# Short first and last token blocks, half a batch of attention ahead of the feed-forward on VectorE, and an in-place maximum in PSUM

## The chip, the cores and the metric

The kernel runs on one core of one Trainium2 chip. The core has TensorE (PE in the profile, with its weight loads shown apart as PEld), VectorE (DVE), ScalarE (ACT), GpSimd (POOL) and SyncE (SP). Each takes its instructions in the order in which they were issued and waits on semaphores. The metric is the device time of one launch in microseconds (us).

## The reference

The inputs are q, k and v, each of 8 batches, 8 heads, 576 positions and 64 features in float32, and two matrices, `w_in` (512 x 2048) and `w_out` (2048 x 512). What is computed, cut to what matters:

```
mask   = abs(pos_q - pos_k) <= 32
scores = where(mask, q @ k.T / sqrt(64), -1e9)
attn   = softmax(scores) @ v                      # per batch and head
x      = attn, heads side by side                 # 4608 tokens x 512
h      = x @ w_in                                 # 4608 x 2048
g      = h if h >= 1, 0 if h <= -1, else (h+1)**2 / 4
out    = g @ w_out                                # 4608 x 512, float32
```

Both kernels use g = min(r, 1) * max(h, r) with r = relu((h+1)/2).

## The kernel before

**Attention.** Two heads make a pair `i` (32 pairs, 4 to a batch); two pairs make a group of four heads, `m` (16 groups, 2 to a batch). `load_qk(m)` fetches q and k of a group on POOL's DMA queue, which also converts float32 to bf16. A partition of `qn` holds nine successive positions of a head, so one row in DRAM is 2304 bytes; `kn` is fetched 64 features at a time, rows of 256 bytes, and so is v (`load_v(i)`, into `vz`, whose other half stays zero). `relay(m)` on POOL reorders `qn` into `qj`. `tpose(m, t)` turns five or four 128 x 128 pieces of `qj` (t = 0, 1) or of `kn` (t = 2, 3) on PE; ACT copies q to `qT`, and DVE copies k into the block-diagonal tile `kz`. `scores(i, g)` multiplies three blocks of 64 keys by the up to 128 queries that can see them, takes exp on ACT and multiplies by the band mask `maskp` on POOL, giving `pt`. `pv(i, hf)` computes for one half (288 positions) the sums of the weights, `dn`, and the weighted v, `nm`, on PE; ACT makes 1/dn with Ln and Exp (`lr`, `rc`), and DVE multiplies (`mul`) into `xT`, the transposed x of all tokens.

**Feed-forward.** Nine blocks of 512 tokens, 16 steps each. In step f PE makes `hp`, 128 of the 2048 features for the block's tokens (four matmuls of 512 columns); ACT makes `rr` = r; DVE writes the maximum of `hp` and `rr` to `yy` in SBUF (L248) and then min(rr, 1) * `yy` to `gT` (L249). In the same step PE does four of the 64 matmuls by `w_out` of the block before (`op`); every fourth step ACT copies a finished `op` to `osb`, and SP's queue stores it.

**Order.** All engines run in program order, written out in one loop over steps `a`. `att_s`, `att_x` and `att_r` say at which step a score group, a transpose, a `pv` or a relay is done; `loads` does so for later loads. The feed-forward begins at step OFF = 29, so 29 steps of attention alone come before it. `hp` and the tiles shared by `tp` and `sc` have two PSUM buffers each, `nm` and `dn` one. PE's order within a step is hp, scores, op, transpose, pv.

Of the kernel before, what the change touches and what calls it, by code (L numbers as in the profile page):

```python
# [15 lines left out]
def kernel(  # L16
# [14 lines left out]

    nc = tc.nc
# [5 lines left out]
    TB = 512  # L38
    NBLK = NT // TB

# [4 lines left out]
    def pcol(c, qq):  # L45
        return qq if c % 2 == 0 else S + qq - 32

    PW = 2 * S - 64
    GROUPS = [(0, 2, 4), (6, 8, 1), (3, 5, 7)]
# [5 lines left out]
    ptp = ctx.enter_context(tc.tile_pool(name="ptp", bufs=3))  # L55
# [18 lines left out]
    vz = [const.tile([128, NC, 128], BF, name=f"vz{i}") for i in range(8)]  # L74
# [5 lines left out]

    def load_qk(m):
        b, qd = divmod(m, 2)
        qn[m] = qkn.tile([128, 2, S], BF, name="qn")
        kn[m] = qkn.tile([128, NC, 2, D], BF, name="kn")
        for g in range(2):
            h0 = 4 * qd + 2 * g
            nc.gpsimd.dma_start(out=qn[m][64 * g:64 * g + 64],
                                in_=q[b, h0:h0 + 2].rearrange("h (p j) d -> p h (j d)", j=NC))
        for g in range(2):
            for h in range(2):  # L90
                nc.gpsimd.dma_start(out=kn[m][64 * g:64 * g + 64, :, h],  # L91
                                    in_=k[b, 4 * qd + 2 * g + h].rearrange("(c p) d -> p c d", p=64))

    def load_v(i):
        b, hp = divmod(i, H // 2)
        for h in range(2):
            nc.gpsimd.dma_start(  # L97
                out=vz[i % 8][64 * h:64 * h + 64, :, 64 * h:64 * h + 64],
                in_=v[b, 2 * hp + h].rearrange("(c p) d -> p c d", p=64))

    nc.scalar.preload_act_table_set("natural_log_exp_and_others")
    load_qk(0)
    for t in kz:
        nc.vector.memset(t.rearrange("p c h r -> p (c h r)").bitcast(FP), 0.0)
    for i in range(8):
        nc.vector.memset(vz[i].rearrange("p c d -> p (c d)").bitcast(FP), 0.0)  # L106
    make_identity(nc, ident)
    for i in range(4):
        load_v(i)
    load_qk(1)  # L110
# [3 lines left out]
    for h in range(2):  # L114
        r = slice(64 * h, 64 * h + 64)
        nc.gpsimd.memset(ones2[r, r], 1.0)
        nc.gpsimd.affine_select(out=mask1[r], in_=mask1[r], compare_op=ALU.is_ge, fill=0.0, base=0,
                                channel_multiplier=-1, pattern=[[1, 128]])
        nc.gpsimd.affine_select(out=mask1[r], in_=mask1[r], compare_op=ALU.is_ge, fill=0.0, base=64,
                                channel_multiplier=1, pattern=[[-1, 128]])  # L120
    for c in range(NC):
        q0, q1 = qrange(c)
        j0 = q0 - (64 * c - 32)
        nc.vector.tensor_copy(maskp[:, pcol(c, q0):pcol(c, q0) + q1 - q0], mask1[:, j0:j0 + q1 - q0])
    nc.gpsimd.dma_start(out=w_in, in_=moe_w_in.rearrange("(ko ki) f -> ki ko f", ki=128))
    load_qk(2)
    for i in range(4, 8):
        load_v(i)
    nc.gpsimd.dma_start(out=w_out, in_=moe_w_out.rearrange("(ko ki) f -> ki ko f", ki=128))


    qj, qT = {}, {}

    def relay(m):

        qj[m] = qjp.tile([128, NC, 2, D], BF, name="qj")
        nc.gpsimd.tensor_copy(qj[m].rearrange("p j h d -> p h j d"),  # L137
                              qn[m].rearrange("p h (j d) -> p h j d", d=D))
# [3 lines left out]
    def tpose(m, t):  # L142

        src, (j0, j1) = (qj if t < 2 else kn)[m], TJ[t % 2]
        ps = ps_s.tile([128, 5, 128], BF, name="tp", tag="sc")
        if t == 0:
            qT[m] = qtp.tile([128, 2, S], BF, name="qT")
        for j in range(j0, j1):
            nc.tensor.transpose(ps[:, j - j0], src[:, j].rearrange("p h d -> p (h d)"), ident)  # L149
        n = j1 - j0  # L150
        if t < 2:
            for g in range(2):
                nc.scalar.copy(  # L153
                    qT[m][:, g].rearrange("d (p j) -> d p j", j=NC)[:, :, j0:j1],
                    ps[:, :n].rearrange("d j (g p) -> d g p j", g=2)[:, g])
        else:
            for h in range(2):
                for g in range(2):
                    r = slice(64 * h, 64 * h + 64)
                    nc.vector.tensor_copy(kz[2 * (m % 2) + g][r, j0:j1, h],  # L160
                                          ps[r, :n].rearrange("d c (g p) -> d g c p", g=2)[:, g])
# [3 lines left out]
    def scores(i, g):  # L165
# [5 lines left out]
        first = None  # L171
        for c in GROUPS[g]:
            q0, q1 = qrange(c)
            nc.tensor.matmul(ps[:, off:off + q1 - q0], kz[2 * (m % 2) + gg][:, c].rearrange("d h r -> d (h r)"),  # L174
                             qT[m][:, gg, q0:q1], start=True, stop=True)
            if first is None:
                first = pcol(c, q0)
            off += q1 - q0
        seg = slice(first, first + off)

        nc.scalar.activation(pt[i][:, seg], ps[:, :off], AF.Exp, scale=D ** -0.5)  # L181
        nc.gpsimd.tensor_mul(pt[i][:, seg], pt[i][:, seg], maskp[:, seg])  # L182

    def pv(i, hf):
# [3 lines left out]
        o0, o1 = max(lo, 32), min(hi, S - 32)  # L188
        nc.tensor.matmul(dn, ones2, pt[i][:, lo:hi], start=True, stop=False)  # L189
        nc.tensor.matmul(dn[:, o0 - lo:o1 - lo], ones2, pt[i][:, pcol(1, o0):pcol(1, o1)], start=False, stop=True)  # L190
# [6 lines left out]
        for n, (c, q0, q1) in enumerate(parts):  # L197
            nc.tensor.matmul(nm[:, q0 - lo:q1 - lo], vz[i % 8][:, c], pt[i][:, pcol(c, q0):pcol(c, q1)],  # L198
                             start=n == 0, stop=n == len(parts) - 1, skip_group_check=True)

# [8 lines left out]
        return mul  # L209


    A0 = 9
    att_s, att_x, att_r = {}, {}, {}
    for m in range(NP // 2):
        for t in range(4):
            att_x[8 * m + 2 * t] = ("t", m, t)
        att_r[8 * m - 1] = m
    for i in range(NP):
        for g in range(3):
            att_s[A0 + 4 * i + g] = (i, g)  # L220
        for hf in range(2):
            att_x[A0 + 4 * i + 4 + 2 * hf] = ("v", i, hf)
    OFF = A0 + 4 * 3 + 6 + 2
    loads = {}
    for m in range(3, NP // 2):
        loads.setdefault(8 * m - 16, []).append((load_qk, m))
    for i in range(8, NP):
        loads.setdefault(4 * i - 14, []).append((load_v, i))

    gT = {}  # L230
    mul = None
    for a in range(-1, OFF + 16 * (NBLK + 1)):
        mm = a - OFF
        blk, f = divmod(mm, 16)
        for fn, arg in loads.get(a, []):
            fn(arg)
        if 0 <= mm and blk < NBLK:
            if f == 0:
                gT[blk] = gtp.tile([128, 16, TB], BF, name="gT")
            hp = ps_h.tile([128, TB], FP, name="hp")  # L240
            for kk in range(4):
                nc.tensor.matmul(hp, w_in[:, kk, 128 * f:128 * f + 128], xT[:, kk, TB * blk:TB * blk + TB],  # L242
                                 start=kk == 0, stop=kk == 3)

            rr = ewp.tile([128, TB], FP, name="rr")
            yy = ewp.tile([128, TB], FP, name="yy")
            nc.scalar.activation(rr, hp, AF.Relu, scale=0.5, bias=0.5)  # L247
            nc.vector.tensor_max(yy, hp, rr)  # L248
            nc.vector.scalar_tensor_tensor(gT[blk][:, f], rr, 1.0, yy, op0=ALU.min, op1=ALU.mult)  # L249
        if mul:  # L250
            mul()
            mul = None
        if a in att_s:
            scores(*att_s[a])
        if 1 <= blk <= NBLK and mm >= 0:
            tt, f0 = divmod(f, 4)
            if f0 == 0:
                op = ps_o.tile([128, DM], FP, name="op")
            for ff in range(4 * f0, 4 * f0 + 4):
                nc.tensor.matmul(op, gT[blk - 1][:, ff, 128 * tt:128 * tt + 128], w_out[:, ff],  # L260
                                 start=ff == 0, stop=ff == 15)
            if f0 == 3:
                osb = osp.tile([128, DM], FP, name="osb")
                nc.scalar.copy(osb, op)  # L264
                t0 = TB * (blk - 1) + 128 * tt
                nc.sync.dma_start(out=out[t0:t0 + 128, :], in_=osb)
        if a in att_r:
            relay(att_r[a])
        if a in att_x:
            kind, i, t = att_x[a]  # L270
            if kind == "t":
                tpose(i, t)
            else:
                mul = pv(i, t)
# [30 lines left out]
```

## Time and profile before

| | |
|---|---|
| median of 3 runs | 393.26 us (392.73 to 393.27) |
| the profiled execution | 393.38 us, of which its span is 391.7 us |
| granted TensorE clock, mean | 0.987 |
| busy: PE, DVE, ACT, POOL | 82%, 74%, 56%, 56% of the span |

The span is the time from the first to the last recorded event; 1.68 us of the profiled execution lie around it. [...] In rows of the profile `out<-in` names tiles, `x` is a count, and what stands in square brackets is the engine's idle time ahead of the instruction and what ended it.

### The profile page before, as it was taken

What the parts mean: (1) busy time and instruction counts of PE and PEld (TensorE: products, weight loads), DVE (VectorE), ACT (ScalarE), POOL (GpSimd) and SP (SyncE); (2) the same over time, 40 slices, a digit from 0 to 9 for tenths busy, and PEclk for the clock granted to TensorE, in tenths of its full rate; (3) what the DMA queues carried; (4) which work ended last, traced back from release to release, by engine and by line L of the source; (5) the groups of instructions that cost most, each with busy time, mean ns of one, the idle gap of its engine ahead of it and who ended that gap; (6) DMA issues with size and microseconds to landing.
All of it is one profiled execution on the core that took longest, in us unless ns stands there. A gap on an engine that the chain in (4) does not pass through costs nothing.

```text
span 391.7 us, 6070 instructions
## 1 busy us (share of the span) xinstructions
PE 322.4 (82%) x2136; PEld 177.9 (45%) x2176; DVE 289.0 (74%) x501; ACT 219.8 (56%) x469; POOL 219.9 (56%) x288
## 2 busy tenths in 40 slices
PE   0000765677699999999999999999999999999995
PEld 0000554444355555555555555555555544444442
DVE  6100332699899999999999999999998877787720
ACT  1000564666677767675867777776766644434421
POOL 8947889996776858694958768642422200000000
PEclk9999995899999999999999999999999999999999
DMA  9999996992939678794939395830000100101012
GB/s 81 99 195 141 172 163 47 73 78 18 77 26 120 77 71 93 67 96 51 104 42 104 45 128 65 83 43 27 28 28 28 54 28 27 54 28 52 29 55 80
DMA packets 88190, 28.18 MB, mean 72 GB/s; under 512 B 76896, under 2 KB 83040, under 8 KB 88160
## 3 DMA queue, kind: packets, MB, share of 16 engines
q0 software_dynamic: 82976, 18.36, 53.2%
q1 hardware_dynamic: 5184, 9.44, 6.4%
q8 instruction: 17, 0.28, 0.3%
q14 instruction: 13, 0.11, 0.1%
HBM read 36.70 MB, written 9.44 MB: 118 GB/s over the span
## 4 chain that ended last, share of the span: by engine, by line
PE 71%; POOL 11%; DVE 9%; DMA 3%; issue 2%; ACT 2%; another core or an unknown queue 1%; ACTq 0%; POOLq 0%
PE op L260 30%; PE hp L242 28%; DMA w_in<-in_moe_w_in_dram 3%; POOL vz L97 3%; PE nm L198 3%; DVE gT L249 3%; PE tp L149 3%; POOL pt L182 3%; PE sc L174 3%; DVE yy L248 3%; POOL kn L91 3%; PE dn L189 2%; PE dn L190 2%; DVE vz L106 1%; DVE xT L208 1%
## 5 line engine op out<-in xcount | busy, mean ns | idle before, releaser
L242 PE MATMUL hp<-xT,w_in 128*128 128x512 bf16 x555 | 146.0, 379 | 4.2 <-DVE xT L208 3.0
L260 PE MATMUL op<-w_out,gT 128*128 128x512 bf16 x557 | 142.3, 379 | 0.7
L249 DVE SCALAR_TENSOR_TENSOR gT<-rr,yy 128x512 bf16<-128x512 f32 x144 | 130.3, 905 | 5.1
L182 POOL TENSOR_TENSOR pt<-pt,maskp 128x352 bf16<-128x352 bf16 (+1 forms) x96 | 85.6, 907 | 79.2 <-ACT pt L181 78.8
L247 ACT ACTIVATE rr<-hp 128x512 f32<-128x512 f32 x144 | 86.1, 598 | 76.7 <-PE hp L242 71.6
L248 DVE TENSOR_TENSOR yy<-hp,rr 128x512 f32<-128x512 f32 x144 | 99.2, 689 | 26.7 <-ACT rr L247 24.4
L260 PEld LDWEIGHTS <-gT 128*128 128x128 bf16 x576 | 53.5, 98 | 51.7
L242 PEld LDWEIGHTS <-w_in 128*128 128x128 bf16 x576 | 51.9, 98 | 43.2 <-issue 0.2
L97 POOL DMA_DIRECT2D vz<-in_v_dram x64 | 48.7, 773 | 8.2 <-DMA w_in<-in_moe_w_in_dram 7.4
L160 DVE COPY kz<-tp 64x320 bf16<-64x320 bf16 (+1 forms) x128 | 33.2, 298 | 25.8 <-PE tp L149 25.3
L149 PE MATMUL tp<-ident,qj 128*128 128x128 bf16 x144 | 15.2, 242 | 44.6 <-POOL qj L137 43.8
L153 ACT COPY qT<-tp 128x320 bf16<-128x320 bf16 (+1 forms) x64 | 24.8, 454 | 47.9 <-PE tp L149 47.7
L91 POOL DMA_DIRECT2D kn<-in_k_dram x64 | 47.9, 791 | 0.9 <-PE tp L149 0.9
L181 ACT ACTIVATE pt<-sc 128x352 bf16<-128x352 f32 (+1 forms) x96 | 45.0, 468 | 2.0 <-PE sc L174 1.8
L208 DVE TENSOR_TENSOR xT<-nm,rc 128x288 bf16<-128x288 f32 x64 | 28.8, 449 | 16.8 <-ACT rc L204 16.8
L203 ACT ACTIVATE lr<-dn 128x288 f32<-128x288 f32 x64 | 26.5, 414 | 19.8 <-PE dn L190 19.8
L174 PEld LDWEIGHTS <-kz 128*128 128x128 bf16 x288 | 25.0, 104 | 25.6 <-issue 6.4
L149 PEld LDWEIGHTS <-qj 128*128 128x128 bf16 x144 | 10.6, 108 | 52.9 <-POOL qj L137 49.4
L174 PE MATMUL sc<-qT,kz 128*128 128x128 bf16 (+1 forms) x288 | 33.2, 228 | 1.6 <-ACT pt L181 1.2
L198 PE MATMUL nm<-pt,vz 128*128 128x128 bf16 (+2 forms) x320 | 27.7, 221 | 7.5 <-DVE xT L208 7.5
L264 ACT COPY osb<-op 128x512 f32<-128x512 f32 x36 | 21.1, 587 | 19.4 <-PE op L260 16.6
L198 PEld LDWEIGHTS <-vz 128*128 128x128 bf16 x320 | 22.2, 103 | 17.8 <-issue 12.5
(26 smaller groups left out, 158.8 us busy)
## 6 DMA issues: line engine op xcount, KB each, us to landing
out_dram<-osb SPq DMA_DIRECT2D x36, 256.0 KB, 2.0
qn<-in_q_dram POOLq DMA_DIRECT2D x32, 144.0 KB, 3.6
kn<-in_k_dram POOLq DMA_DIRECT2D x64, 72.0 KB, 4.4
vz<-in_v_dram POOLq DMA_DIRECT2D x64, 72.0 KB, 3.0
w_in<-in_moe_w_in_dram POOLq DMA_DIRECT2D x1, 2048.0 KB, 12.8
w_out<-in_moe_w_out_dram POOLq DMA_DIRECT2D x1, 2048.0 KB, 15.0
```

Source lines behind the costliest of these rows:

```text
L91: nc.gpsimd.dma_start(out=kn[m][64 * g:64 * g + 64, :, h], in_=k[b, 4 * qd + 2 * g + h].rearrange("(c p) d -> p c d", p=64))
L97: nc.gpsimd.dma_start(out=vz[i % 8][64 * h:64 * h + 64, :, 64 * h:64 * h + 64], in_=v[b, 2 * hp + h].rearrange("(c p) d -> p c d", p=64))
L149: nc.tensor.transpose(ps[:, j - j0], src[:, j].rearrange("p h d -> p (h d)"), ident)
L174: nc.tensor.matmul(ps[:, off:off + q1 - q0], kz[2 * (m % 2) + gg][:, c].rearrange("d h r -> d (h r)"), qT[m][:, gg, q0:q1], start=True, st ...
L181: nc.scalar.activation(pt[i][:, seg], ps[:, :off], AF.Exp, scale=D ** -0.5)
L182: nc.gpsimd.tensor_mul(pt[i][:, seg], pt[i][:, seg], maskp[:, seg])
L198: nc.tensor.matmul(nm[:, q0 - lo:q1 - lo], vz[i % 8][:, c], pt[i][:, pcol(c, q0):pcol(c, q1)], start=n == 0, stop=n == len(parts) - 1, ski ...
L242: nc.tensor.matmul(hp, w_in[:, kk, 128 * f:128 * f + 128], xT[:, kk, TB * blk:TB * blk + TB], start=kk == 0, stop=kk == 3)
L247: nc.scalar.activation(rr, hp, AF.Relu, scale=0.5, bias=0.5)
L248: nc.vector.tensor_max(yy, hp, rr)
L249: nc.vector.scalar_tensor_tensor(gT[blk][:, f], rr, 1.0, yy, op0=ALU.min, op1=ALU.mult)
L260: nc.tensor.matmul(op, gT[blk - 1][:, ff, 128 * tt:128 * tt + 128], w_out[:, ff], start=ff == 0, stop=ff == 15)
```

## The change

1. **Block sizes.** The nine blocks of 512 tokens become `sizes = [256] + [512] * 8 + [256]`.
2. **Attention ahead of the feed-forward.** Instead of 29 loop steps, a hand-written stretch does the first half (`hf = 0`) of the four pairs of batch 0. Relays, the copies into `kz` (`zfill`) and the mask multiplications run on DVE there, and during the first block (t = 0, steps 0 to 15) too; from block 1 on, relays and mask multiplications are on POOL again. Attention of batch 0's second half and of batch 1 is spread over block 0, batch b (2 to 7) over block b - 1.
3. **Score groups** become (0, 2, 4), (1, 3) and (6, 8, 5, 7), so that the first half needs only the first two.
4. **Loads.** For groups m = 0 to 3 k is fetched like q, in rows of 2304 bytes, relayed (`kj`), transposed to `kT` and copied to `kz`. A group's q (and k) is one DMA over 128 partitions instead of two of 64. v is fetched per group. `w_in` comes in two pieces (columns 0 to 511 early, the rest later, four DMAs each) and `w_out` in four. Later q and k loads are issued up to 38 steps ahead.
5. **Maximum in place.** DVE writes the maximum over `hp` in PSUM (L363); `yy` is gone, and L364 reads `hp`. The `hp` buffer comes free after L364 instead of after the maximum.
6. `zero` clears only the halves of `kz` and `vz` that no load fills, and clears `vz` later.

The core of the diff:

```
-    GROUPS = [(0, 2, 4), (6, 8, 1), (3, 5, 7)]
+    GROUPS = [(0, 2, 4), (1, 3), (6, 8, 5, 7)]
...
+    LONG = 4
     def load_qk(m):
...
+            if nm == "kn" and m >= LONG:
+                t = dst[m] = qkn.tile([128, NC, 2, D], BF, name="kn", tag="kn")
...
+            t = dst[m] = qkn.tile([128, 2, S], BF, name=nm, tag=nm)
+            rows = src[b, 4 * qd:4 * qd + 4].rearrange("(h g) s d -> h (g s) d", g=2)
+            nc.gpsimd.dma_start(out=t, in_=rows.rearrange("h (x j) d -> x h (j d)", j=NC))
...
+    load_v(0, 0, 5)
+    load_v(1, 0, 5)
+    load_w_in(0, 512)
     load_qk(2)
+    load_qk(3)
+    load_v(0, 5, NC)
+    load_v(1, 5, NC)
+    load_w_in(512, DFF)
+    load_v(2)
+    load_v(3)
+    for n in range(4):
+        load_w_out(n)
...
+    def zfill(m, g, eng):
+        for h in range(2):
+            r = slice(64 * h, 64 * h + 64)
+            eng.tensor_copy(kz[2 * (m % 2) + g][r, :, h], kT[m][r, g].rearrange("d (c r) -> d c r", r=64))
...
-        nc.gpsimd.tensor_mul(pt[i][:, seg], pt[i][:, seg], maskp[:, seg])
+        eng.tensor_mul(pt[i][:, seg], pt[i][:, seg], maskp[:, seg])
...
+    sizes = [256] + [512] * 8 + [256]
...
+        eng = V if t == 0 else P
...
-            nc.vector.tensor_max(yy, hp, rr)
-            nc.vector.scalar_tensor_tensor(gT[blk][:, f], rr, 1.0, yy, op0=ALU.min, op1=ALU.mult)
+            nc.vector.tensor_max(hp[:, :n], hp[:, :n], rr[:, :n])
+            nc.vector.scalar_tensor_tensor(gT[t][:, f, :n], rr[:, :n], 1.0, hp[:, :n], op0=ALU.min, op1=ALU.mult)
```

**Order on POOL's queue at the start.** Before, from the load of `w_in` on (`vz_112` to `vz_115` are the v tiles of batch 1, `qj` the relayed q):

```order
L125 DMA w_in<-in_moe_w_in_dram 128x4x2048
L87 DMA qn<-in_q_dram 64x2x576 x2
L91 DMA kn<-in_k_dram 64x9x64 x4
L97 DMA vz_112<-in_v_dram 64x9x64 x2
L97 DMA vz_113<-in_v_dram 64x9x64 x2
L97 DMA vz_114<-in_v_dram 64x9x64 x2
L97 DMA vz_115<-in_v_dram 64x9x64 x2
L129 DMA w_out<-in_moe_w_out_dram 128x16x512
L137 COPY qj<-qn 128x2x9x64 x2
```

In the changed kernel the same stretch, from the first piece of `w_in` on (`vz_108` and `vz_109` are v of batch 0, `vz_110` and `vz_111` of batch 1; the `qn` after `w_out` is that of group 4, the first of batch 2):

```order
L117 DMA w_in<-in_moe_w_in_dram 64x2x512 x4
L99 DMA qn<-in_q_dram 128x2x576
L99 DMA kn<-in_k_dram 128x2x576
L99 DMA qn<-in_q_dram 128x2x576
L99 DMA kn<-in_k_dram 128x2x576
L111 DMA vz_108<-in_v_dram 64x4x64 x4
L111 DMA vz_109<-in_v_dram 64x4x64 x4
L117 DMA w_in<-in_moe_w_in_dram 64x2x1536 x4
L108 DMA vz_110<-in_v_dram 64x18x64 x2
L108 DMA vz_111<-in_v_dram 64x18x64 x2
L121 DMA w_out<-in_moe_w_out_dram 128x4x512 x4
L99 DMA qn<-in_q_dram 128x2x576
```

The relay no longer stands behind `w_out` on POOL, and q of group 4 stands behind everything else.

**Order on DVE ahead of the feed-forward.** Before, after the memsets (`mask_99` is the band of one block, `tp` the transposed k):

```order
L124 COPY maskp<-mask_99 128x96
L124 COPY maskp<-mask_99 128x128 x7
L124 COPY maskp<-mask_99 128x96
L160 COPY kz_104<-tp 64x5x64
L160 COPY kz_105<-tp 64x5x64
```

In the changed kernel, after the memsets of `kz`:

```order
L169 COPY qj<-qn 128x2x9x64
L169 COPY kj<-kn 128x2x9x64
L198 COPY kT<-tp 128x128x5
L198 COPY kT<-tp 128x128x4
L203 COPY kz_104<-kT 64x9x64 x2
L267 COPY maskp<-mask_99 128x96
L267 COPY maskp<-mask_99 128x128 x7
L267 COPY maskp<-mask_99 128x96
L220 TENSOR_TENSOR pt<-pt,maskp 128x352
L220 TENSOR_TENSOR pt<-pt,maskp 128x256
L169 COPY qj<-qn 128x2x9x64
```

Relays, `zfill` and mask multiplications have come to DVE, between what it did already.

**Order on DVE in the first block.** Before, at its start:

```order
L248 TENSOR_TENSOR yy<-hp,rr 128x512
L249 SCALAR_TENSOR_TENSOR gT<-rr,yy 128x512
L248 TENSOR_TENSOR yy<-hp,rr 128x512
L249 SCALAR_TENSOR_TENSOR gT<-rr,yy 128x512
L208 TENSOR_TENSOR xT<-nm,rc 128x288
L160 COPY kz_106<-tp 64x4x64
```

In the changed kernel, around step 8:

```order
L248 TENSOR_TENSOR xT<-nm,rc 128x288
L220 TENSOR_TENSOR pt<-pt,maskp 128x256
L169 COPY qj<-qn 128x2x9x64
L363 TENSOR_TENSOR hp<-hp,rr 128x256
L364 SCALAR_TENSOR_TENSOR gT<-rr,hp 128x256
L220 TENSOR_TENSOR pt<-pt,maskp 128x480
```

The `qj<-qn` here is the relay of group 4: every later maximum of block 0 is queued behind its wait for that load.

More of the change, by code (lines that the diff above doesn't have):

```diff
@@ L225, with flush @@
[L225 to L228, printed above, removed]
-    gT = {}
[L231 to L237, printed above, removed]
+        muls.append(mul)
+    muls = []
+    def flush():
+        while muls:
+            muls.pop(0)()
@@ L278 @@
+        for e in rel.get(a, []):
+            relay(*e, eng)
+        for e in es:
+            if e[0] == "t":
+                tpose(e[1], e[2])
+        for m in zf.get(a, []):
+            for g in range(2):
+                zfill(m, g, eng)
+        for e in es:
+            if e[0] == "v":
+                pv(e[1], e[2])
 _INS = ['q', 'k', 'v', 'moe_w_in', 'moe_w_out']
```

288 lines of the change are left out of this document (182 added, 106 removed).

## The prediction

> **What bounds the kernel now.** I read the page's engine shares and slices first, then busy times by stretch, then the start and the end in order of time, then the groups by shape for prices. The slices show PE idle for four of 40 and not full for seven more; from the twelfth on it is full to the end, while DVE is close to full from the ninth to the 30th.
>
> ```profile
> PE 322.4 (82%) x2136; PEld 177.9 (45%) x2176; DVE 289.0 (74%) x501; ACT 219.8 (56%) x469; POOL 219.9 (56%) x288
> PE   0000765677699999999999999999999999999995
> DVE  6100332699899999999999999999998877787720
> GB/s 81 99 195 141 172 163 47 73 78 18 77 26 120 77 71 93 67 96 51 104 42 104 45 128 65 83 43 27 28 28 28 54 28 27 54 28 52 29 55 80
> ```
>
> By stretch, with the copies of finished `op` tiles (16 are four blocks) in the last row:
>
> ```profile
> core 0: us, PE busy (x) PEld busy (x) DVE busy (x) ACT busy (x) POOL busy (x), PEclk, DMA share, GB/s
> 40.00:70.00 30.00, 19.53 (x156) 15.32 (x155) 9.22 (x31) 17.35 (x45) 27.91 (x37) 0.84 1.13 129
> 70.00:107.00 37.00, 24.87 (x203) 14.58 (x206) 31.98 (x58) 23.69 (x55) 32.24 (x40) 0.99 0.78 59
> 111.00:255.00 144.00, 141.51 (x1007) 79.16 (x1026) 134.29 (x226) 103.54 (x224) 107.46 (x137) 1.00 0.73 80
> 111.00:255.00 144.00, 9.38 (x16) 1.00 0.73 80
> ```
>
> So there are four parts: nothing on PE to 39.4, attention alone with POOL as the bound (27.91 of 30 us), block 0 (70 to 107) bound by DVE with POOL beside it, and from 107 a stretch in which PE is the bound. The start in order of time shows why PE waits: the relay stands on POOL behind the issue of every load up to `w_out`.
>
> ```profile
> 36.92 1.21 POOL L129 DMA_DIRECT2D w_out<-in_moe_w_out_dram  x1
> 38.18 2.23 POOL L137 COPY qj<-qn 128x1152 bf16<-128x1152 bf16 x2
> 39.37 1.14 PE L149 MATMUL tp<-ident,qj 128*128 128x128 bf16 x9 [39.37 <-POOL qj L137]
> 387.90 0.59 ACT L264 COPY osb<-op 128x512 f32<-128x512 f32 x1 [2.87 <-remote]
> ```
>
> PE's last `op` ends at 387.9; what follows it, one copy and one store, takes 3.8 us of the 391.7 us span. A change is worth here what it takes from the 107 us ahead of the full stretch, less what it adds to PE's own work or to that stretch.
>
> **The part in which PE is full.** Its steps without attention:
>
> ```profile
> 346.21 1.03 PE L242 MATMUL hp<-xT,w_in 128*128 128x512 bf16 x4
> 347.32 0.60 ACT L247 ACTIVATE rr<-hp 128x512 f32<-128x512 f32 x1 [0.33 <-PE hp L242]
> 347.94 1.03 PE L242 MATMUL hp<-xT,w_in 128*128 128x512 bf16 x4
> 347.95 0.69 DVE L248 TENSOR_TENSOR yy<-hp,rr 128x512 f32<-128x512 f32 x1 [0.31 <-ACT rr L247]
> 348.75 0.69 DVE L249 SCALAR_TENSOR_TENSOR gT<-rr,yy 128x512 bf16<-128x512 f32 x1
> ```
>
> A step of eight matmuls of 512 columns takes 347.94 - 346.21 = 1.73 us, 0.216 each, and a block 27.7. With a batch of attention beside it a block took 144/4 = 36.0, so a batch costs PE 8.3. After the change PE has, from block 1 on: `hp` of 4352 tokens, 8.5 x 64 x 0.216 = 117.5; all `op`, 576 x 0.216 = 124.4; six batches (2 to 7), 50. That is 292 us. Check on before: from 107 on eight blocks of `hp` (110.6), the same `op` and some 5.4 batches (45) give 280, and the trace has 387.9 - 107 = 281.
>
> **The change part by part.** Prices come from these rows (mean ns of one is the second number after the bar; the last three are minimum/median/maximum, while POOL multiplies, while POOL is idle, and for the maximum while POOL multiplies):
>
> ```profile
> L249 DVE SCALAR_TENSOR_TENSOR gT<-rr,yy 128x512 bf16<-128x512 f32 x144 | 130.3, 905 | 5.1
> L182 POOL TENSOR_TENSOR pt<-pt,maskp 128x352 bf16<-128x352 bf16 x64 | 56.6, 886 | 59.8 <-ACT pt L181 59.5
> L208 DVE TENSOR_TENSOR xT<-nm,rc 128x288 bf16<-128x288 f32 x64 | 28.8, 449 | 16.8 <-ACT rc L204 16.8
> L137 POOL COPY qj<-qn 128x1152 bf16<-128x1152 bf16 x16 | 18.2, 1144 | 0.0
> L160 DVE COPY kz<-tp 64x320 bf16<-64x320 bf16 x64 | 17.7, 315 | 25.6 <-PE tp L149 25.3
> L160 DVE COPY kz<-tp 64x256 bf16<-64x256 bf16 x64 | 15.5, 281 | 0.3
> 3.44 4.79 DVE L106 MEMSET vz<- 128x576 f32 x8
> 18.32 1.34 DVE L124 COPY maskp<-mask 128x96 bf16<-128x96 bf16 x9 [10.09 <-POOL mask L119]
> L249 DVE SCALAR_TENSOR_TENSOR gT<-rr,yy x15: 691/693/1441, 77.1 to 105.9; 128x512 bf16<-128x512 f32 x15
> L249 DVE SCALAR_TENSOR_TENSOR gT<-rr,yy x23: 691/692/693, 321.1 to 359.0; 128x512 bf16<-128x512 f32 x23
> L248 DVE TENSOR_TENSOR yy<-hp,rr x15: 675/684/692, 76.4 to 105.1; 128x512 f32<-128x512 f32 x15
> ```
>
> Two float32 operands cost (692 - 449)/(512 - 288) = 1.085 ns an element plus 137, so 415 ns at 256 columns. bf16 copies on DVE cost (315 - 281)/64 = 0.53 ns an element. No row has the moved operations on DVE; I price them by this slope: a relay 281 + 0.53 x 896 = 756 ns (between 281, the small copy, and POOL's 1144), a `zfill` of 576 elements 451 (281 to 692), a mask multiplication of 352 columns 137 + 0.53 x 352 = 324, of 256 273, of 480 391 (up to 1.085 an element, 519 for the first, or POOL's 886). The `kT` copies scatter their output, so I take the dear slope: 831 and 692 (cheap: 485 and 417).
>
> *Start.* The q of group 0 lands when one DMA of twice the size has come:
>
> ```profile
> 1.34 1.39 POOL L87 DMA_DIRECT2D qn<-in_q_dram  x2 [0.81 <-POOLq L289]
> DMA to landing us min/median/max: 3.2/3.7/13.0
> 24.00:30.00 6.00, 0.00 (x0) 0.00 (x0) 0.00 (x0) 0.00 (x0) 0.00 (x0) 1.00 1.07 216
> 32.00:36.00 4.00, 0.00 (x0) 0.00 (x0) 0.00 (x0) 0.00 (x0) 3.52 (x6) 1.00 2.38 152
> ```
>
> 1.34 + 3.2 + 147 KB more at 216 GB/s (`w_in` alone; v alone ran at 152) = 5.3 us. From there DVE has, up to the first `hp`: five relays 3.8, four `kT` copies 3.0, eight `zfill` 3.6, `maskp` 1.3, eight multiplications 2.4, `vz` memsets 4.8, four `xT` 1.8: 20.7 us. It waits where the chain goes over PE and ACT (transposes of q and k, exp after `zfill`, `nm` behind the last `xT`); six such places of 0.5 to 1 us, say 4. The first `hp` comes at 30 (27 to 34), against 71 before.
>
> *Block 0.* Per 256 columns DVE has 16 x 2 x 415 = 13.3; 16 multiplications, 5.5; eleven `xT`, 4.9; four `kT` copies 3.0; eight `zfill` 3.6; five relays 3.8; eight `kz` copies 2.4: 36.5 us; with some waiting and some of these prices too high I take 37 (33 to 42). PE's share is about 17 us at full clock. The whole stage thus ends at 67 instead of 107. Block 1 has, on DVE, 16 x 2 x 0.69 + 8 x 0.45 + 16 x 0.3 = 30.5 plus waits, against 29 on PE (6.9 of `op` only): 3 us over PE's time.
>
> *Loads.* Ahead of the relay of group 4 (step 8 of block 0) the queue moves, as bf16, 2.36 MB of q and k, 4.19 of weights, 0.29 of q at 216 GB/s and 1.18 of v at 152: 31.7 + 7.8 us. From 2.8 us on, plus some 5 in which POOL issues eight small v loads and the masks slower than they move, plus 1 to land, that is 48.5 us. DVE reaches this relay at 30 + 24 = 54 (the first nine steps' share of the sum), so the load is hidden with 5 us to spare. `w_in`'s second piece lands near 33, and step 4 is at 41. From group 4 on k costs as before.
>
> *Maximum in PSUM.* L249 loses its second SBUF operand; while POOL multiplied it reached 1441 ns, the maximum, with one operand in PSUM, never over 692. I price both at 692 everywhere; 144 x (905 - 692) = 31 us of DVE time go, nearly all under a full PE, so only block 1 gains: at the old price its DVE sum is 3.4 higher, and the time 372. [...] What DVE's write into PSUM costs no row shows; reading it costs nothing (L248 and L249 both 692), so I take 0. The buffer is held longer: `hp` begins at 346.21 and L249 would free it at 349.44, while the next use begins at 346.21 + 3.46 = 349.67. That leaves 0.2 us in blocks 7 and 8; I add 1 us (0 to 4).
>
> *Last block.* PE is full to its end either way, and the copy and store behind it stay: 0, for which the cover is PE's own queue of `op`. Score groups and `zero` move no PE time.
>
> *Sum.* 30 + 37 + 292 + 3 + 1 + 3.8 = 366.8 us of span; with 1.7 around it as before, 368.5 us. This is against the profiled execution's 393.38, 0.1 above the median of 393.26.
>
> **The rivals.**
>
> *Loads come late.* DVE stands at the relay of group 4, and all of block 0's rest behind it. At the mean rate of the first six slices, 142 GB/s, the 8.0 MB take 57 us, which is a stall of 4 us: 372. If POOL can't issue while DVE runs its new copies (relays, `zfill`, `maskp`: 8.7 us up to the first `hp`, 5.9 in the steps after), the load comes up to 14.6 us later, a stall of 9: 378. Against it: POOL issued `w_in` in its usual time beside the `maskp` copies at 18.3. [...]
>
> *PE is slow in block 0.* From 40 to 70 PE made 156 matmuls in 30 us at a clock of 0.84, in waits of the same kind. Block 0 has some 250; at that rate it takes 48 us: 379. For it: clock and short chains; against it: POOL, the bound there, is out of the chain, and from 70 to 107 the clock was 0.99 with PE two thirds busy.
>
> *DVE's write into PSUM is dear, and the kernel gets slower.* DVE is busy 134.29/64 = 2.10 us a step beside a batch; less 0.21 that is 1.89 of PE's 2.25, and 1.38 of 1.73 without attention. So x us more per step cost nothing up to 0.35; beyond it 16 x + 112 (x - 0.35) decides, and at x = 0.5, a maximum of 1.2 us instead of 0.69, the 25 us are gone: 393. For it only that no row shows such a write.
>
> *It does nothing*, since the start is given back as waiting for loads or attention later: PE's 292 us would have to grow by 25, and the half batch that a block needs last is done three steps or more before that block.
>
> **Chances and range.** Forecast (358 to 377) 0.64; late loads 0.16; slow PE 0.12; dear write 0.06, half of it past 394; nothing 0.02. The range takes the first three: 358 is a first `hp` at 27, block 0 in 33 and neither the 3 nor the 1; 382 is slow PE with a late start. A difference under 0.2% can't be told from none. Faster 0.94, same 0.02, slower 0.04.
>
> **What would show it.** Right: first transpose near 6 us, first `hp` near 30, first `op` near 67, PE full from there, L364 at 692 or less beside POOL's multiplications, last `op` near 363. Wrong: DVE idle at the relay before block 0's step 9, waiting for a DMA; a clock near 0.5 in block 0; L363 over 1 us; PE waiting at `hp` for L364 in blocks 2 to 8.

## The result, and the profile after

The changed kernel takes 372.81 us (median of four runs, 372.19 to 372.99) against 393.23 (392.73 to 393.27) for the kernel before: 0.9481 of it, with a 95% interval of 0.9464 to 0.9497. That is 20.4 us less; the prediction said 368.5, 24.8 less. The profiled execution took 372.99 us with a span of 371.1. (Of the run with a second `nm` buffer, below, one of six executions took 699.02 us, with a span of 697.1 at a granted clock of 1.00, for a reason that nothing here shows; its numbers leave this one out.)

The page's shares and two of its slices, after:

```profile
PE 326.5 (88%) x2203; PEld 185.3 (50%) x2240; DVE 286.3 (77%) x563; ACT 218.7 (59%) x453; POOL 168.1 (45%) x220
PE   1446674598989999999999999999999999999995
DVE  3667877868898888888797979797878887877660
```

PE is idle in no slice and full from about the ninth of 40 instead of the twelfth. DVE has nearly the work of before (286.3 against 289.0 us), POOL 52 us less. The start, `hp`'s first matmuls, the end of block 0 and the last copy, in order of time (the number after the start is the busy time; the last bracket is the idle time ahead and who ended it):

```profile
5.58 0.59 DVE L169 COPY qj<-qn 128x1152 bf16<-128x1152 bf16 x1 [1.56 <-DMA qn<-in_q_dram]
6.22 1.14 PE L184 MATMUL tp<-ident,qj 128*128 128x128 bf16 x9 [6.22 <-DVE qj L169]
...
30.77 0.85 PE L358 MATMUL hp<-xT,w_in 128*128 128x256 bf16 x3
...
74.43 1.06 PE L376 MATMUL op<-w_out,gT 128*128 128x512 bf16 x2
...
367.37 0.58 ACT L380 COPY osb<-op 128x512 f32<-128x512 f32 x1 [2.91 <-PE op L376]
```

So the span has four pieces: 30.8 to the first `hp`, 43.6 to the first `op` (block 0), 293.0 to the last copy, 3.7 behind it. Predicted were 30, 37, 296 and 3.8: block 0 is 6.6 us longer, the rest 3 us shorter. Busy times in the first two pieces:

```profile
core 0: us, PE busy (x) PEld busy (x) DVE busy (x) ACT busy (x) POOL busy (x), PEclk, DMA share, GB/s
5.50:30.80 25.30, 11.56 (x85) 8.09 (x86) 16.51 (x43) 8.98 (x20) 21.21 (x36) 1.00 1.16 140
30.80:74.40 43.60, 27.01 (x255) 20.60 (x255) 33.64 (x88) 24.91 (x61) 20.66 (x27) 0.95 1.41 149
```

No engine is full in either. DVE, which was to be the bound, is idle for 8.8 us of the first stretch and 10.0 of block 0. The groups by shape hold the prices that had no row before (after the bar: us in all, mean ns):

```profile
L363 DVE TENSOR_TENSOR hp<-hp,rr 128x512 f32<-128x512 f32 x128 | 89.5, 699 | 39.8 <-ACT rr L362 38.0
L363 DVE TENSOR_TENSOR hp<-hp,rr 128x256 f32<-128x256 f32 x32 | 13.8, 431 | 14.6 <-ACT rr L362 14.4
L203 DVE COPY kz<-kT 64x576 bf16<-64x576 bf16 x16 | 7.1, 446 | 0.3
L169 DVE COPY qj<-qn 128x1152 bf16<-128x1152 bf16 x6 | 2.8, 473 | 1.6 <-DMA qn<-in_q_dram 1.6
L220 DVE TENSOR_TENSOR pt<-pt,maskp 128x352 bf16<-128x352 bf16 x8 | 2.7, 335 | 3.9 <-ACT pt L219 3.9
```

The relay costs 473 ns (priced 756), the other rows are within 4% of their prices, and the maximum that DVE writes into PSUM costs 699 ns: 7 more than the 692 taken for it.

Where block 0's idle time on DVE comes from is seen in single steps. PE and DVE around one of them:

```profile
45.50 0.43 DVE L363 TENSOR_TENSOR hp<-hp,rr 128x256 f32<-128x256 f32 x1
45.97 0.42 DVE L364 SCALAR_TENSOR_TENSOR gT<-rr,hp 128x256 bf16<-128x256 f32 x1
46.31 0.45 DVE L248 TENSOR_TENSOR xT<-nm,rc 128x288 bf16<-128x288 f32 x1
...
46.81 0.66 PE L239 MATMUL nm<-pt,vz 128*128 128x64 bf16 x5 [1.38 <-DVE xT L248]
47.26 1.06 PE L358 MATMUL hp<-xT,w_in 128*128 128x256 bf16 x4
...
48.77 0.43 DVE L363 TENSOR_TENSOR hp<-hp,rr 128x256 f32<-128x256 f32 x1 [1.77 <-ACT rr L362]
```

PE stands at `nm` for 1.38 us, since the one `nm` buffer comes free only with DVE's `xT`, which stands on DVE behind this step's maximum and product. The next `hp` stands on PE behind `nm`, so that DVE then waits 1.77 us for it, over ACT. PE and DVE wait for each other in turn; neither has to be busy all the time for that.

### The profile page after: what moved, and what is told of

Its sections match the earlier page's. It is cut to its first block, busy times and chain, and to the rows that moved or that the text cites. A ratio compares the mean times of both kernels' runs of the same rounds, so it can differ in the third digit from the quotient of the medians.

```text
span 371.1 us, 6161 instructions
## 1 busy us (share of the span) xinstructions
PE 326.5 (88%) x2203; PEld 185.3 (50%) x2240; DVE 286.3 (77%) x563; ACT 218.7 (59%) x453; POOL 168.1 (45%) x220
## 4 chain that ended last, share of the span: by engine, by line
PE 77%; DVE 15%; ACT 3%; issue 2%; DMA 2%; POOL 0%; DVEq 0%; ACTq 0%; POOLq 0%
PE op L376 32%; PE hp L358 30%; PE nm L239 4%; PE tp L184 4%; PE sc L215 3%; DVE hp L363 3%; DVE gT L364 3%; DVE xT L248 2%; DVE kz L203 2%; ACT rr L362 2%; DMA kn<-in_k_dram 2%; PE dn L229 2%; PE dn L230 1%; DVE kz L190 1%; DVE kT L198 1%
## 5 line engine op out<-in xcount | busy, mean ns | idle before, releaser
L358 PE MATMUL hp<-xT,w_in 128*128 128x512 bf16 (+1 forms) x618 | 149.8, 362 | 4.4 <-DVE xT L248 2.5
L363 DVE TENSOR_TENSOR hp<-hp,rr 128x512 f32<-128x512 f32 (+1 forms) x160 | 103.2, 645 | 54.3 <-ACT rr L362 52.3
L362 ACT ACTIVATE rr<-hp 128x512 f32<-128x512 f32 (+1 forms) x160 | 88.6, 554 | 90.4 <-PE hp L358 74.8
L364 DVE SCALAR_TENSOR_TENSOR gT<-rr,hp 128x512 bf16<-128x512 f32 (+1 forms) x160 | 101.4, 633 | 5.6
L220 POOL TENSOR_TENSOR pt<-pt,maskp 128x352 bf16<-128x352 bf16 (+2 forms) x72 | 63.5, 885 | 92.2 <-ACT pt L219 81.8
L219 ACT ACTIVATE pt<-sc 128x352 bf16<-128x352 f32 (+2 forms) x96 | 44.5, 468 | 10.8 <-PE sc L215 10.6
L94 POOL DMA_DIRECT2D kn<-in_k_dram x48 | 35.9, 773 | 6.1 <-DMA w_out<-in_moe_w_out_dram 2.4
L239 PE MATMUL nm<-pt,vz 128*128 128x128 bf16 (+2 forms) x320 | 27.5, 219 | 11.3 <-DVE xT L248 8.3
L196 ACT COPY qT<-tp 128x640 bf16<-128x640 bf16 (+1 forms) x32 | 23.5, 740 | 16.0 <-PE tp L184 14.6
L239 PEld LDWEIGHTS <-vz 128*128 128x128 bf16 x320 | 21.7, 102 | 19.6 <-issue 13.5
L244 ACT ACTIVATE rc<-lr 128x288 f32<-128x288 f32 x64 | 28.4, 443 | 2.0
L108 POOL DMA_DIRECT2D vz<-in_v_dram x28 | 24.4, 887 | 0.9 <-PE tp L184 0.7
```

What stands on the lines that cost most here:

```text
L94: nc.gpsimd.dma_start(out=t[64 * g:64 * g + 64, :, h], in_=src[b, 4 * qd + g + 2 * h].rearrange("(c r) d -> r c d", r=64))
L220: eng.tensor_mul(pt[i][:, seg], pt[i][:, seg], maskp[:, seg])
L239: nc.tensor.matmul(nm[:, q0 - lo:q1 - lo], vz[i // 2 % 4][:, i % 2, c], pt[i][:, pc(c, q0):pc(c, q0) + q1 - q0], start=n == 0, stop=n == l ...
L358: nc.tensor.matmul(hp[:, :n], w_in[:, kk, 128 * f:128 * f + 128], xT[:, kk, t0:t0 + n], start=kk == 0, stop=kk == 3)
L362: nc.scalar.activation(rr[:, :n], hp[:, :n], AF.Relu, scale=0.5, bias=0.5)
L363: nc.vector.tensor_max(hp[:, :n], hp[:, :n], rr[:, :n])
```

## The experiments

Times are medians with all runs' range; ratios, with 95% intervals, are to the kernel before on the same chip (393.2 to 393.4 us).

### The maximum back in SBUF

```
+            yy = ewp.tile([128, 512], FP, name="yy")
-            nc.vector.tensor_max(hp[:, :n], hp[:, :n], rr[:, :n])
+            nc.vector.tensor_max(yy[:, :n], hp[:, :n], rr[:, :n])
```

(and the product reads `yy`.)

> The changed kernel with the maximum back in SBUF (yy), everything else as changed. My theory: DVE's 31 us of contention lie under a full PE and only block 1 pays them, some 3 us, less what the earlier release of hp gives back: 373 to 377 us, DVE busy some 25 us more. Rival: the in-place maximum is what made most of the 20 us, 380 or more. Second rival: holding hp longer costs what the contention cost, no difference or faster than 372.8.

Measured: 380.3 us (379.41 to 384.3), 0.9695 [0.9661, 0.9728], 7.5 more than the changed kernel, beyond the 4 us that the theory gave at most. The copies of finished `op` tiles show where. The third, the 19th and the last, first of the changed kernel and then of this one:

```profile
117.55 0.59 ACT L380 COPY osb<-op 128x512 f32<-128x512 f32 x1
...
258.78 0.58 ACT L380 COPY osb<-op 128x512 f32<-128x512 f32 x1
```

```profile
119.91 0.59 ACT L381 COPY osb<-op 128x512 f32<-128x512 f32 x1
...
264.64 0.59 ACT L381 COPY osb<-op 128x512 f32<-128x512 f32 x1
...
373.96 0.59 ACT L381 COPY osb<-op 128x512 f32<-128x512 f32 x1 [2.91 <-PE op L377]
```

The first `op` comes at the same time (74.3 against 74.4), so block 0, where POOL has no multiplications, doesn't care. 2.4 us are lost by the third copy, which comes early in block 2, that is in block 1; 3.5 in the next 16 copies, four blocks (144.73 against 141.23 us); 0.7 later; 6.6 in the trace. The product costs 866 ns in the mean, up to 1656 beside POOL, where the changed kernel's never exceeds 690. PE's waits at `nm` for `xT` grow from 8.3 to 13.2 us. The stretch that was taken for full has such waits too: a longer DVE operation ahead of `xT` reaches PE there. One step in block 3:

```profile
154.36 1.65 DVE L365 SCALAR_TENSOR_TENSOR gT<-rr,yy 128x512 bf16<-128x512 f32 x1
155.93 0.44 DVE L248 TENSOR_TENSOR xT<-nm,rc 128x288 bf16<-128x288 f32 x1
...
156.43 0.40 PE L239 MATMUL nm<-pt,vz 128*128 128x64 bf16 x5
```

`nm` begins as soon as the late `xT` has ended, 0.37 us behind `dn`'s second matmul (at 156.06). In blocks 2 to 5 of the changed kernel this distance is 0.11 us in all 32 places; here most are longer, by 0.13 to 0.27 us, 3.6 us in all, which is the whole of the loss in these four blocks. Little of this is counted as idle time: successive matmuls overlap in the profile (in the changed kernel `dn`'s second matmul lasts 0.27 us, and `nm` begins 0.11 us behind its start), and from 140 to 220 us PE is busy for 79.03 us here and for 79.42 in the changed kernel. So PE looks full. The product in blocks 1 to 4 (minimum/median/maximum in ns) with the maximum in SBUF, the same in the changed kernel, and PE's wait with the maximum in SBUF (us in all, times, longest):

```profile
L365 DVE SCALAR_TENSOR_TENSOR gT<-rr,yy x63: 691/693/1656, 75.7 to 218.5; 128x512 bf16<-128x512 f32 x63
```

```profile
L364 DVE SCALAR_TENSOR_TENSOR gT<-rr,hp x66: 686/686/690, 75.7 to 219.5; 128x512 bf16<-128x512 f32 x66
```

```profile
PE nm L239 <- DVE xT L248: 13.2, 17, 1.6
```

### The kernel before with the maximum in PSUM alone

```
-            nc.vector.tensor_max(yy, hp, rr)
+            nc.vector.tensor_max(hp, hp, rr)
```

> The kernel before with the in-place maximum alone. My theory: only block 0, from 70 to 107 us, is bound by DVE; 16 steps lose 0.21 us each of contention, so 389 to 391.5 us, and DVE's busy time falls by some 31 us while PE's full stretch from 107 on keeps its 281 us. Rival: DVE bounds more of the kernel than the slices show, 10 us or more.

Measured: 392.07 us (391.86 to 393.15), 0.9971 [0.9961, 0.9982], 1.2 less, somewhat under what the theory gave. In the four blocks beside attention DVE is busy 116.04 us instead of 134.29 and PE exactly as long as before:

```profile
111.00:255.00 144.00, 141.51 (x1007) 79.13 (x1026) 116.04 (x225) 103.63 (x224) 107.46 (x137) 1.00 0.73 80
```

Over the whole kernel DVE is busy for 261.7 us instead of 289.0, 27.3 less, and 1.2 us are won; in the new order 18.6 us less (286.3 against 304.9) are worth 7.5. What DVE saves isn't what counts, then, but whether its longer product makes an `xT` late: in the kernel before, with the maximum in SBUF, `nm` begins some 0.11 us behind `dn` in 31 of the 32 places of blocks 1 to 4 and 0.18 in the other. Which of the moved steps made it otherwise in the new order was not tried.

### The short last block ahead of a long one

```
-    sizes = [256] + [512] * 8 + [256]
+    sizes = [256] + [512] * 7 + [256, 512]
```

> The changed kernel with its short last block taken from the end: the last two blocks are 256 and then 512 tokens instead of 512 and 256, so that 64 op matmuls instead of 32 run after the last hp. My theory: PE's work is the same and PE is full to the end, so the short last block is worth nothing; with 512 tokens of hp beside the op of 256, 16 steps are bound by DVE at 1.42 us against 1.30 on PE: 372.8 to 375. Rival: the short last block shortens the end by the 32 matmuls, 6.9 us: 379.7.

Measured: 377.35 us (376.51 to 378.6), 0.9595 [0.9578, 0.9613], 4.5 more, past the 375 that the theory gave at most; its 1.42 us a step was too little. Since the short block's `op` is half as much, a step of the long block after it has only 1.30 us of matmuls (six of 0.216), but takes 1.61. Every second maximum in it:

```profile
337.43 0.70 DVE L363 TENSOR_TENSOR hp<-hp,rr 128x512 f32<-128x512 f32 x1 [0.46 <-ACT rr L362]
...
343.85 0.70 DVE L363 TENSOR_TENSOR hp<-hp,rr 128x512 f32<-128x512 f32 x1 [0.46 <-ACT rr L362]
```

Four steps take 6.42 us. A buffer of `hp` goes through matmuls, `rr`, maximum and product before the next use, and two buffers allow two steps in that time: 3.21 us. PE stands for L364 to free `hp` every second step:

```profile
338.90 1.02 PE L358 MATMUL hp<-xT,w_in 128*128 128x512 bf16 x3 [0.43 <-DVE gT L364]
```

(1.61 - 1.30) x 16 = 5.0 us is the loss. So this is the price of the place, not of a long last block, and the longer hold of `hp` that the change brings shows here; in the changed kernel's blocks without attention, at 1.73 us a step, it hides.

### k of all groups in short rows

```
-    LONG = 4
+    LONG = 0
```

(with the relays, and the copies into `kz`, that belong to it.)

> The changed kernel with k of all groups fetched in rows of 256 bytes and copied from PSUM into kz, with no relay of k, no kT and no zfill. My theory: the loads are hidden, and what DVE saves on relay, kT copies and zfill of four groups (some 15 us) is about what the 32 kz copies cost (10 us), while k of group 0 lands 2 to 3 us later and POOL issues 9 us longer: 370 to 377. Rival: the long rows are what makes the early start, first hp 8 us later: 380 or more.

Measured: 375.2 us (374.92 to 376.46), 0.9544 [0.9529, 0.9559], 2.4 more. The front gets shorter, since the relays and scattered copies of k fall away (first `hp` at 28.0), but block 0 takes 51.3 us (first `op` at 79.3). Now loads do come late: PE stands at `w_in`'s second piece, and DVE 3.7 us at the relay of a q that hasn't landed.

```profile
43.21 0.38 PE L352 MATMUL hp<-xT,w_in 128*128 128x256 bf16 x2 [3.06 <-DMA w_in<-in_moe_w_in_dram]
```

Long rows seem to pay, then, by what stands behind k in the queue rather than by k; no run separates the two.

### A second `nm` buffer ahead of block 1

```
-        nm = ps_n.tile([128, HALF], FP, name="nm")
+        if two[0]:
+            two[0] += 1
+        if two[0] % 2:
+            nm = ps_o.tile([128, HALF], FP, name="nm2", tag="op")
+        else:
+            nm = ps_n.tile([128, HALF], FP, name="nm")
...
+        if t > 0:
+            two[0] = 0
```

(`two` starts at 2, so that every second `nm` ahead of block 1 lies in a buffer of `op`.)

> The changed kernel with a second PSUM buffer for nm up front and in block 0 (every other nm lies in an op bank, which has no use before block 1). My theory: block 0 took 43 us instead of 37 because PE, in order, stands at nm until DVE has read the nm before (xT), and hp, rr and the next maximum stand behind it; without that wait block 0 is 3 to 6 us shorter: 367 to 370 us, and DVE's idle time in 31 to 74 falls from some 9 us by as much. Rival: block 0 is slow because PE's clock is low there (0.66 in one stretch of 5 us), which a buffer doesn't mend: 372 to 373.

Measured: 370.99 us (368.78 to 372.8, five executions), 0.942 [0.9393, 0.9448], 1.8 less than the changed kernel: a gain, but smaller than the theory's 3 to 6 us.

### A third `qT` buffer

```
-    qtp = ctx.enter_context(tc.tile_pool(name="qtp", bufs=2))
+    qtp = ctx.enter_context(tc.tile_pool(name="qtp", bufs=3))
```

> The changed kernel with three buffers each for qT and kT instead of two. My theory: the 1.2 us for which ACT stands at the first qT copy of group 2, whose buffer scores of group 0 still read at step 1, go, 1 to 1.6 us: 371 to 372. Rival: another engine is behind anyway at that place, no difference.

Measured: 370.33 us (369.81 to 372.47), 0.9426 [0.9405, 0.9448], 2.5 less, more than the theory gave. But in its profile the first `op` is at 74.5, no earlier: what the second step gains is lost again by the end of block 0, in which the granted clock is 0.88 instead of 0.95. The gain in the trace (1.4 us from the first `op` to the last copy) lies in PE's clock, below.

### Both buffers

> Both the second nm buffer in block 0 and three qT buffers. My theory: the two waits are at different steps and the gains add: 365.5 to 369. Rival (low clock): 371 to 373.

Measured: 369.61 us (369.47 to 371.18), 0.9402 [0.9384, 0.9419]. This is the fastest version, 3.2 us below the changed kernel, and still slower than the theory's range. Its first `op` is at 71.26, 3.2 earlier, but the rest takes 294.2 us instead of 293.0. Of the 3.2 us, 1.75 are there already at the first `hp` (29.02 against 30.77), since PE's waits at `nm` ahead of it go too; block 0 itself is only 1.4 us shorter. PE's wait at `nm` in block 0 of the changed kernel, and the two longest waits of PE for DVE that are left in the kernel with both buffers beside the relay's (us in all, times, longest):

```profile
PE nm L239 <- DVE xT L248: 6.4, 6, 1.6
```

```profile
PE hp L366 <- DVE xT L253: 4.0, 3, 1.9
PE sc L215 <- DVE kz L203: 2.5, 1, 2.5
```

They were 2.5 and 1.4 us in the changed kernel. So PE, freed from one wait for DVE, mostly stands at another, and DVE is still idle for 7.0 us of the 42.3.

The first 5 us behind the first `op` in three traces (the changed kernel, a third `qT` buffer, both buffers; the third number from the end is the granted clock):

```profile
74.00:79.00 5.00, 5.00 (x32) 3.06 (x31) 1.73 (x3) 3.42 (x8) 0.88 (x2) 0.68 0.01 3
```

```profile
74.00:79.00 5.00, 4.85 (x43) 3.04 (x43) 2.98 (x6) 4.34 (x10) 2.06 (x3) 1.00 0.02 3
```

```profile
71.00:76.00 5.00, 5.00 (x26) 2.88 (x25) 1.39 (x2) 2.94 (x7) 0.85 (x1) 0.50 0.01 3
```

By estimate, the 5 us times what the granted clock is short of 1.00, PE loses 1.6 us at 0.68, nothing at 1.00 and 2.5 at 0.50; from the first `op` to the last copy the three take 293.0, 291.6 and 294.2 us. So 1.2 of the 3.2 us that this trace has won by the first `op` are given back behind it, through the low clock.

### Block 0's mask multiplications on POOL

```
-                scores(e[1], e[2], eng)
+                scores(e[1], e[2], P)
```

> The changed kernel with the mask multiplications of block 0 back on POOL; those up front stay on DVE, as do all relays. My theory: DVE sheds 5 us, but the multiplications stand on POOL behind the issue of group 4's and 5's loads, which wait for w_out's transfers until 45 to 50 us, so the first pv of block 0 comes some 12 us later: 380 to 388. Rival: DVE is what bounds block 0, so it gets shorter by 3 to 5 us: 368 to 370.

Measured: 384.11 us (383.03 to 385.0), 0.9753 [0.9731, 0.9775], 11.3 more. The size is as the theory had it. The reason is seen in one place, on POOL and on PE:

```profile
45.46 0.73 POOL L94 DMA_DIRECT2D kn<-in_k_dram  x1 [1.00 <-DMA w_out<-in_moe_w_out_dram]
46.25 2.14 POOL L220 TENSOR_TENSOR pt<-pt,maskp 128x480 bf16<-128x480 bf16 x2
...
47.39 0.40 PE L229 MATMUL dn<-pt,ones 128*128 128x288 bf16 x1 [11.11 <-POOL pt L220]
```

The changed kernel's first multiplication of block 0 is on DVE at 33.78. POOL's comes at 46.25, since issues of loads stand ahead of it and wait for earlier transfers. PE stands 11.11 us for it, which is nearly the whole 13.5 us by which block 0 grows. What POOL takes for a multiplication (1.07 us against 0.40) is small beside its place in the queue.

### Relays and masks on POOL at the front too

```
-    relay(0, 0, V)
+    relay(0, 0, P)
...
-        eng = V if t == 0 else P
+        eng = P
```

(for all relays and mask multiplications; q and k have four buffers, the copies into `kz` stay on DVE.)

> The changed kernel with relays and mask multiplications on POOL again, ahead of the feed-forward and in block 0 (the copies into kz and the attention order stay; q and k get a fourth buffer each, since POOL would otherwise wait for its own relay). Theory: that the start moves at all comes from VectorE taking the relays, because POOL's stand behind every load that is issued before them. POOL's last issue ahead of them was at 38.5 and took 0.74 us, so the first relay starts at about 39 instead of 5.6, the first hp comes at 39 + 25 + some 4 for POOL's dearer relays and masks = 66 to 72, block 0 takes some 55 to 60 as in the run with the masks alone on POOL, and 293 + 5 follow: 415 to 430, slower than the kernel before, which did this attention without the feed-forward's chain beside it. Rival: the early start and the shape of the front matter little, and a front that finds all loads landed catches up in block 0: 395 to 405.

Measured: 402.44 us (401.77 to 404.6), 1.0234 [1.0208, 1.026]: slower than the kernel before. The theory was near on the start (66 to 72) and wrong on block 0 (55 to 60); the rival's time was right:

```profile
38.93 1.14 POOL L169 COPY qj<-qn 128x1152 bf16<-128x1152 bf16 x1
...
64.27 0.49 PE L358 MATMUL hp<-xT,w_in 128*128 128x256 bf16 x3
```

```profile
64.00:105.00 41.00, 26.96 (x260) 20.26 (x260) 27.60 (x66) 25.46 (x62) 37.05 (x43) 0.88 0.85 66
```

The first `hp` comes 33.5 us later. But block 0 then takes 40.7 us, 2.9 less than with the work on DVE, though POOL is busy for 37.05 us of that window: the early loads have been issued by then, and little stands ahead of its multiplications. So the change earns its time in the start. In block 0 the run with the masks on POOL and this one together say that DVE has to do POOL's work there because POOL's queue is full of loads then.

### More work for DVE in block 0

```
+            if t == 0:
+                V.tensor_copy(scr, maskp)
```

> The changed kernel with one more bf16 copy of 128 x 1088 on VectorE (written to a tile that nobody reads) in each of the 16 steps of block 0, behind the multiplication into gT; at the relay's price of 0.45 to 0.47 us that is 7.3 us of VectorE time. Theory A: block 0 goes by VectorE's queue, and PE's waits at nm, tp and sc are waits for results that stand in that queue, so that nearly all of the added time appears: +5.5 to +7.3, 378 to 380. Theory B: block 0 is bound by the chain of handoffs over PE and ACT, VectorE is idle for 9.5 of its 43 us, and most of the copies go into those gaps: +0 to +3, 373 to 376.

Measured: 377.72 us (376.85 to 379.53), 0.961 [0.9585, 0.9634], 4.9 more, between the two theories. In the trace the first `op` comes at 80.7; block 0 grows by 6.5 us for 16 copies of 0.438 us, 7.0 in all.

```profile
L367 DVE COPY scr<-maskp x16: 434/438/697, 33.6 to 77.3; 128x1088 bf16<-128x1088 bf16 x16
```

DVE, idle for 10 us there, hides almost nothing of it in the trace, and some 2 us in the medians: its operations lie in the loop with PE, so most of what is put into it appears.

### Half of the copies into `kz` on ACT, with both buffers

```
-                zfill(m, g, eng)
+                zfill(m, g, nc.scalar if g else V)
```

> The kernel with three qT buffers and a second nm buffer (369.6), and with one of the two copies per half group into kz (those of g = 1 in block 0) on ScalarE instead of VectorE. It takes 4 x 0.46 = 1.8 us from VectorE in block 0, runs beside the other half, and lets the scores, which PE waits for, begin up to 0.9 us earlier twice; ScalarE is busy 27 of 43 us there. Theory A (VectorE's queue bounds block 0): 1 to 2.5 us less, 367 to 368.6. Theory B (the handoffs bound it, and rr stands behind ScalarE's new copies): no change or up to 1 us more, 369.3 to 370.6.

Measured: 372.13 us (370.27 to 374.37), 0.9467 [0.9432, 0.9502]: no gain, rather a loss on the 369.61 of the kernel that it starts from, and above both theories. ACT takes 670 ns for a copy that costs DVE 446; the first `op` comes at 72.0 instead of 71.3. The runs scatter too far to size the loss.

### The kernel before with two relays on DVE

```
-        nc.gpsimd.tensor_copy(qj[m].rearrange("p j h d -> p h j d"),
+        (nc.vector if m < 2 else nc.gpsimd).tensor_copy(qj[m].rearrange("p j h d -> p h j d"),
```

> The kernel before with the first two relays (m = 0 and 1) on VectorE and nothing else changed. Theory: the start is held by POOL's queue as a whole, not by the relay in it; the first mask multiplications stand on POOL behind the same issues (up to w_out at 38.1) and behind two more groups' issues of q and k (4.2 us and a wait of 0.9), so they begin at about 42.5 to 43.3 instead of 45.43, PE stops after the first scores, and the gain is 2 to 4 us: 389 to 391. Rival: the relay alone holds the start; then PE begins near 20 instead of 39.4, and a good part of these 19 us appears: 375 to 385.

Measured: 393.02 us (392.46 to 394.29), 0.9996 [0.9986, 1.0005]: no difference. The theory's chain is there, but even its 2 us are missing:

```profile
20.03 1.14 PE L149 MATMUL tp<-ident,qj 128*128 128x128 bf16 x9 [20.03 <-DVE qj L137]
...
42.46 3.32 POOL L182 TENSOR_TENSOR pt<-pt,maskp 128x352 bf16<-128x352 bf16 x4
...
43.36 0.40 PE L189 MATMUL dn<-pt,ones 128*128 128x288 bf16 x1 [13.91 <-POOL pt L182]
```

PE starts 19.3 us earlier and then stands 13.91 us for the masks, which come 3 us earlier than before. By the first `hp` 0.7 us of it are left (70.3 against 71.0), since POOL, the bound of that stretch, then waits 2.58 us for a transfer of `w_out` and at 56.89 is where it was at 56.94 before. An early start needs more than the relays on DVE: the masks that PE then waits for stand in the same queue.

## Why the prediction was right, and where it was off

- **Start: right in the sum, wrong in its parts.** Predicted 30 for the first `hp`, measured 30.8. DVE's work from the first relay on was priced at 20.7 us and took 16.5: the relays are cheaper, successive operations overlap by some 0.1 us in the profile (0.08 where `xT` begins at 46.31 behind L364 at 45.97), and a relay, an `xT` and a memset come only after the first `hp` has begun. Waits were put at 4 us and are 8.8. That these misses cancel is luck.
- **Block 0: the step that failed.** "With some waiting and some of these prices too high I take 37." The prices were about right: the groups of this stretch add up to 37.4 us, with a relay, an `xT` and a memset more than were counted, but since they overlap, DVE is busy for only 33.6. The waits, for which next to nothing was added, are 10.0 us: 43.6 in all, past the 42 given as the end of its range. A sum over one engine is a lower bound where engines take turns. It is no question of DVE's busy time alone, though it counts: 7.0 us more on DVE cost 6.5 in the trace (4.9 in the medians), while a block 0 with 6 us less DVE work (relays and masks on POOL, where they take longer, loads done) gains only 2.9. A second `nm` buffer and a third `qT` buffer, which take no work away, gain 1.4 us in block 0 and 1.75 ahead of it. So the one `nm` buffer is a place where the turns show, but only a part of the 6.6 us; how the rest divides among the other handoffs was not taken apart.
- **PE's part: 293.0 against 296.** A batch was priced at 8.3 us of PE from the 36.0 us that a block took beside it. In the new order four blocks take 141.2 us, 35.3 each: 7.6 a batch, 4 us less over six batches, so 288. Where 3 us were added for block 1 and 1 for the longer hold of `hp`, there are 5.0, and 3.6 in the trace whose clock stays full (291.6). The hold was looked for in blocks 7 and 8; it shows in block 1, twice, and nowhere else:

```profile
PE hp L358 <- DVE gT L364: 1.0, 2, 0.6
```

- **Maximum in PSUM: effect right, size wrong.** The long products beside POOL's multiplications go: in blocks 1 to 4 they take 1656 ns at most with two SBUF operands, 690 with one in PSUM. Why they are long no run shows. But the sentence that all of it lies "nearly all under a full PE, so only block 1 gains", 3.4 us, fails: it is worth 7.5, of which 2.4 in block 1 and 3.5 in blocks 2 to 5, where a late `xT` reaches PE. DVE's saving was put too high too: 27.3 us in the old order and 18.6 in the new, against 31. In the sum this did no harm, since the forecast had every product at 692 ns anyway.
- **The rivals.** Late loads: not there; the relay of group 4 began at 57.96 with no wait for a DMA, against 54 predicted. The kernel with short rows shows how near it is. Slow PE in block 0: the clock was 0.95 there, which by estimate costs at most 0.05 x 43.6 = 2.2 of the 6.6 us; with 0.88 in the kernel with a third `qT` buffer the block took no longer, but that kernel has a wait less, so that a part isn't excluded. A dear write into PSUM: 7 ns. Doing nothing: no.

The misses, +0.8 - 3 + 6.6 - 0.1, make the 4.3 us by which the span (371.1) stands above the sum of 366.8.

## What to carry to other kernels

Price a stage with alternating engines by its loop, not by its busiest engine: find the buffers and results that each waits for, follow what stands ahead of the operation that frees them, and add that wait per step; a second buffer for one of them can move the wait to the next. Idle time of an engine inside such a loop is little room for more work: 4.9 of 7.0 us appeared. Work that moves off a queue of DMA issues gains by its place, not by its duration, and it has to take the whole chain along: the relays alone were worth nothing in the old order, relays and masks together 33.5 us at the first `hp` of the new one (29.6 in its whole time). What the shorter product gains depends on the surrounding order: 1.2 us in one and 7.5 in another.

## What the hardware showed that was not expected

Behind block 0, in which PE is busy for 27.0 of 43.6 us, the changed kernel's granted clock falls to 0.50 for some microseconds; with a third `qT` buffer it stays at 1.00 there. In windows of 2 us around the start of block 1, first in the changed kernel, then with a third `qT` buffer:

```profile
72.00:74.00 2.00, 0.25 (x1) 0.10 (x1) 1.63 (x6) 0.00 (x0) 0.00 (x0) 0.94 0.00 0
74.00:76.00 2.00, 2.00 (x12) 1.27 (x11) 0.96 (x2) 0.95 (x2) 0.54 (x1) 0.50 0.03 8
76.00:78.00 2.00, 2.00 (x15) 1.24 (x13) 0.42 (x1) 1.49 (x3) 0.32 (x1) 0.70 0.00 0
```

```profile
72.00:74.00 2.00, 0.23 (x2) 0.00 (x0) 1.93 (x7) 0.26 (x1) 0.00 (x0) 1.00 0.00 0
74.00:76.00 2.00, 1.85 (x20) 1.34 (x20) 0.87 (x3) 1.44 (x3) 0.35 (x1) 1.00 0.04 8
```

Both have the same gap of nearly 2 us on PE (1.92 and 1.93 us, the longest there); in the changed kernel the clock is then short of 1.00 by an estimated 0.12 + 1.0 + 0.6 = 1.7 us in all, in the other by nothing. In windows of half a microsecond the changed kernel's clock is 0.78 from 73.5 us, 0.50 in all six from 74.0 to 77.0, 0.81 from 77.0 and 1.00 from 77.5, which makes by estimate some 3.4 us at half clock. With both buffers it is 0.94, 0.50, 0.50, 0.50 and 0.85 in the windows of 2 us from 68 to 78 us; the same sum gives 3.4 us lost, so by estimate 6.8 us at half clock, twice as long. What sets off such a spell, and what its length, no run shows. In block 0 a clock of 0.88 instead of 0.95 went with a block that took no longer, in a kernel that has a wait less there; from the first `op` to the last copy, where PE is the bound, the two traces with such a spell take 1.4 and 2.6 us longer than the one without. Differences of 1 to 2 us between these kernels should be read with that in mind.
